# First batch on keys before values, peaks turned on VectorE, and a planner that also counts GpSimd and open banks

## The chip, the cores and the metric

One core of a Trainium2 chip runs the whole kernel. Its engines are named as the profile names them: PE is TensorE's products, PEld its weight loads, DVE is VectorE, ACT is ScalarE, POOL is GpSimd, SP is the SyncE queue that issues DMAs. The metric is the time of one execution in microseconds (us), the median of three runs.

## What is computed

An attention over 32 memory slots feeds a mixture of 8 experts of which each token uses one. The reference, cut to what matters (8 batches, 8 heads, 576 tokens, 64 channels a head; 4608 tokens of 512 channels; experts 512 to 1024 to 512):

```python
a = softmax(phi, axis=2)                    # over the tokens
k_m = einsum('bhsm,bhsd->bhmd', a, k)       # 32 keys and 32 values a head
v_m = einsum('bhsm,bhsd->bhmd', a, v)
x = softmax(q @ k_m.T / 8) @ v_m            # then tokens by 512 channels
logits = x @ w_gate + modality_bias[modality_id]
e = argmax(logits); gate = softmax(logits)[e]
out = gate * (relu(x @ w1[e]) @ w2[e])
```

## The kernel before

**What is multiplied.** The kernel guesses one expert from the biases, takes every token to choose it, and checks that at the end (`verdict`, L539 to L544, sets a flag; the branch behind it, for other choices, isn't taken in the trace). The value products are folded into the expert: for each batch `vw` = values times w1 (L555), so that hidden = relu(a times vw). Large products run in three terms on numbers split into an upper and a lower part (names ending in h and l): `hidden` (L588) takes xh by vwh, xl by vwh, xh by vwl; `outputs` (L617) takes hh by w2h, hl by w2h, hh by w2l. A batch's tokens come in two parts: part 0 has 4 of 9 column groups (tile `xa`, 256 columns), part 1 has 5 (tile `xb`, 320 columns).

**The steps of one batch**, with the lines of the profile:
- `mem_max` folds phi over the tokens on DVE (L253 to L257). `mem_top` turns the result on PE (L141) and reduces it (L268, `topc`). `mem_exp` spreads the peak over the partitions by products with a broadcast weight (L278), subtracts it on DVE (L284) and takes exp on ACT (L287). `mem_sums` adds the exps up, on POOL for all but batch 0.
- `kv_products` multiplies the exps by keys and values together (L307, 72 products, which the trace shows as 144) and by ones (L315, the sums). `kv_divide` divides (L322 to L334), `mem_turn` turns keys and values on PE (L141) and ACT copies them out (L364, L372). `mem_gate` (L391, L396) makes the gate's weights.
- `q_turn` turns queries in place on DVE (L402). `scores` (L414) writes four banks. `soften` and `normalise` (L441 to L473) run on DVE, with one exp on ACT (L449). `a_split` makes xh on ACT (L482) and xl on DVE (L485).
- `logits` (L502 to L514) and `gate` (L521 to L531) give the gates. `gated` (L630) scales a finished output tile on ACT and frees its bank.

**Where things lie.** PSUM has four single banks named `pe`, taken in turn by hidden, outputs and vw, and two pairs named `pair`. A hidden product's bank comes free when ACT (L597) and DVE (L600) have read it. An output tile holds its bank over 24 products and until L630.

**The first batch** is written out by hand in `plan_first`: one list for all engines, with idle products (`warm`, L154 and L156: nothing is read from them) between the steps. All loads go through the SP queue in the order phi, k, v, q (columns of part 0), q (part 1), the modality, the gate's weights, then w1 and w2 of the guessed expert.

**All later batches** are woven by `weave`. It holds two lists, `attention` (each step with a due time, counted in progress of the products) and `experts` (the products), and a table `TAKES` with a time for each kind on PE and a chain on DVE (D), ACT (A) and POOL (P). It simulates one clock and writes out whichever step can go. So the order on each engine is fixed when the program is built, and every engine runs its own list in that order.

Of the kernel before, what the change touches and what calls it, by code (L numbers as in the profile page):

```python
# [54 lines left out]
def attn_moe(ctx: ExitStack, tc: tile.TileContext, q, k, v, phi, mod_id, w_gate, mod_bias, w1, w2, out):  # L55
# [23 lines left out]
    BUSY = 92, 2  # L79
# [69 lines left out]
    def warm(n, small=False, name="pa"):  # L149
        if n > 0:  # L150
            idle = bank(name)
            for _ in range(n):
                if small:
                    nc.tensor.matmul(idle[0:BL, 0:64], lhsT=busy[:, 0:BL], rhs=busy[:, 0:64], start=True, stop=True)  # L154
                else:
                    nc.tensor.matmul(idle, lhsT=busy[:, 0:P], rhs=busy, start=True, stop=True)  # L156
# [113 lines left out]

    def mem_exp(b):
        ph = phs[b % 2].rearrange("p j (c m) -> p j c m", m=M)
        topc = live["topc", b]
        pe = wk.tile([P, HG, QC * M], F32, name="exp")
        px = pe.rearrange("p j (c m) -> p j c m", m=M)
        pb = bank("mem")
        for g in range(NG):
            nc.tensor.matmul(  # L278
                pb[QP * g:QP * (g + 1), 0:P], lhsT=topc[:, g:g + 1].broadcast_to([P, QP]), rhs=ident,
                start=True, stop=True, tile_position=(0, QP * g),  # L280
            )
        peak = pb[:, 0:P].rearrange("p (j o m) -> p j o m", j=HG, o=1)
# [13 lines left out]
    def kv_products(b):  # L296
# [15 lines left out]
        for j in range(HG):  # L312
            for g in range(NG):
# [3 lines left out]
                    start=True, stop=True, tile_position=(QP * g, M * j),  # L317
                )
# [47 lines left out]
    def values_turn(b, fresh=False):  # L366
        if fresh:
            live["pkv"] = pair_of_banks(0)
        turn(live["pkv"][:, 1, 0:P], live["values", b].rearrange("p g d -> p (g d)"))

    def values_out(b):
        nc.scalar.copy(vT[b].rearrange("p j m -> p (j m)"), live["pkv"][:, 1, 0:P])  # L372
# [11 lines left out]
    def first_values():  # L384
        values_turn(0, True)
# [89 lines left out]
    def a_split(b, part, step=None):  # L475
# [9 lines left out]
        nc.vector.tensor_tensor(l, src, h.bitcast(F32), op=ALU.subtract)  # L485
# [164 lines left out]
    def first_w2(c):  # L650
# [11 lines left out]
        "max": (0.0, "D1.9"), "guess": (0.0, "D0.4"), "top": (0.3, "D0.25"),  # L662
        "exp": (0.35, "D1.5 A0.7"), "first exp": (0.35, "D1.5 A0.7"), "first sums": (0.0, "D1.9"), "sums": (0.0, "P0.5"),
        "vwp": (1.15, ""), "vwu": (0.0, "A1.15"), "vwl": (0.0, "D1.35"),
# [422 lines left out]
```

## Time and profile before

| | |
|---|---|
| runs | 403.18, 403.55, 403.67 us, median 403.55 |
| the profiled execution | 405.46 us, of which the span from the first to the last instruction is 403.6 |
| TensorE clock granted | 0.989 of full speed over the span |
| instructions in the span | 10100, of them 4251 products and 4254 weight loads |

The span of the profiled execution is what all rows below count from; the rest of its 405.46 us, 1.9 us, lies outside. A row of the timeline has the start, the time, engine and line, output and inputs, shapes and count; in brackets stands how long the engine had been idle before and what ended it.

### The profile page before, as it was taken

To read this page: it belongs to the slowest core of one execution; us is meant where nothing else is said; L and a number is where in the kernel's file an instruction comes from. 1 tells how busy PE (TensorE), PEld (TensorE's weight loads), DVE (VectorE), ACT (ScalarE), POOL (GpSimd) and SP (SyncE) were. 2 spreads that over 40 slices of the span, in tenths; PEclk is the share of its full clock that TensorE was granted. 3 is DMA by queue.
4 is the path that set the end of the run, shared out by engine and by line. 5 is a ranking of instruction groups with operands and counts; after the bars stand their busy time and mean duration, and the time that the engine had idled before them with its cause. 6 is when DMAs were issued, how large, how long until landed. Compare 5 with 4: busy or idle time off the path is not lost.

```text
span 403.6 us, 10100 instructions
## 1 busy us (share of the span) xinstructions
PE 387.7 (96%) x4251; PEld 309.4 (77%) x4254; DVE 238.8 (59%) x581; ACT 143.7 (36%) x342; POOL 39.9 (10%) x79
## 2 busy tenths in 40 slices
PE   5989998999999999999999999999999999989994
PEld 5448885889678878787968879688877879678983
DVE  2677745975697556853686457764488437860400
ACT  1245333524243324332443315343342424341410
POOL 3158010002000200011000200002000200000000
PEclk9799999999999999999999999999999999999998
DMA  6999158634641491518411282524501011341112
GB/s 218 325 384 392 52 155 298 223 130 112 209 172 54 137 317 65 209 35 294 164 26 54 64 317 86 206 82 110 179 17 38 26 29 28 131 159 26 28 28 58
DMA packets 28966, 56.90 MB, mean 141 GB/s; under 512 B 3312, under 2 KB 8432, under 8 KB 28912
## 3 DMA queue, kind: packets, MB, share of 16 engines
q1 hardware_dynamic: 28624, 56.16, 41.8%
q8 instruction: 35, 0.57, 0.6%
q14 instruction: 19, 0.16, 0.1%
q10 hardware_dynamic: 288, 0.01, 0.0%
HBM read 37.29 MB, written 18.87 MB: 139 GB/s over the span
## 4 chain that ended last, share of the span: by engine, by line
PE 90%; DVE 3%; ACT 2%; DMA 2%; issue 1%; POOL 1%; ACTq 0%; POOLq 0%
PE pe L617 50%; PE pe L588 23%; PE pair L307 4%; PE pe L555 4%; PE pair L414 3%; DMA ph<-in_phi_dram 2%; PE pair L502 1%; PE pair L156 1%; PE pair L141 1%; DVE hl L600 1%; ACT exp L287 1%; PE pair L278 1%; PE pe L156 1%; ACT hh L597 1%; PE pair L555 1%
## 5 line engine op out<-in xcount | busy, mean ns | idle before, releaser
L617 PE MATMUL pe<-w2h,hh 128*128 128x512 f32 x288 | 117.9, 409 | 0.4 <-DVE hl L600 0.4
L617 PE MATMUL pe<-w2h,hl 128*128 128x512 f32 x288 | 112.6, 391 | 0.0
L617 PE MATMUL pe<-w2l,hh 128*128 128x512 f32 x288 | 110.4, 391 | 0.0
L600 DVE SCALAR_TENSOR_TENSOR hl<-pe,hh 128x256 fp32r<-128x256 f32 (+2 forms) x160 | 58.6, 393 | 53.7 <-ACT hh L597 53.2
L617 PEld LDWEIGHTS pe<-w2h,hh 128*128 128x128 f32 x288 | 54.0, 188 | 25.4 <-issue 12.9
L597 ACT ACTIVATE hh<-pe 128x256 fp32r<-128x256 f32 (+2 forms) x160 | 53.6, 361 | 39.5 <-PE pe L588 39.0
L617 PEld LDWEIGHTS pe<-w2l,hh 128*128 128x128 f32 x288 | 54.0, 188 | 12.0
L617 PEld LDWEIGHTS pe<-w2h,hl 128*128 128x128 f32 x288 | 54.2, 188 | 9.3
L630 ACT ACTIVATE ob<-pe,gates 128x512 f32<-128x512 f32 x36 | 24.7, 689 | 82.4 <-PE pe L617 43.1
L588 PE MATMUL pe<-xbh,vwh 128*128 128x320 f32 x128 | 39.8, 311 | 0.0
L588 PE MATMUL pe<-xbl,vwh 128*128 128x320 f32 x128 | 39.6, 309 | 0.0
L588 PE MATMUL pe<-xbh,vwl 128*128 128x320 f32 x128 | 39.5, 309 | 0.0
L588 PE MATMUL pe<-xah,vwh 128*128 128x256 f32 x128 | 36.9, 291 | 0.2 <-DVE hl L600 0.2
L588 PE MATMUL pe<-xal,vwh 128*128 128x256 f32 x128 | 35.9, 283 | 0.0
L588 PE MATMUL pe<-xah,vwl 128*128 128x256 f32 x128 | 35.3, 283 | 0.0
L253 POOL TENSOR_TENSOR t2sums<-exp 128x512 f32<-128x512 f32 x7 | 9.0, 1286 | 261.8 <-ACT exp L287 261.8
L588 PEld LDWEIGHTS pe<-xah,vwh 128*128 128x128 f32 x128 | 24.4, 191 | 1.4 <-DVE hl L600 0.7
L588 PEld LDWEIGHTS pe<-xal,vwh 128*128 128x128 f32 x128 | 24.5, 191 | 0.3
L588 PEld LDWEIGHTS pe<-xbh,vwh 128*128 128x128 f32 x128 | 24.1, 188 | 0.5 <-issue 0.2
L588 PEld LDWEIGHTS pe<-xbl,vwh 128*128 128x128 f32 x128 | 24.1, 188 | 0.3
L588 PEld LDWEIGHTS pe<-xah,vwl 128*128 128x128 f32 x128 | 24.0, 191 | 0.3 <-issue 0.3
L588 PEld LDWEIGHTS pe<-xbh,vwl 128*128 128x128 f32 x128 | 24.1, 188 | 0.0
(117 smaller groups left out, 428.7 us busy)
## 6 DMA issues: line engine op xcount, KB each, us to landing
kv_sb<-in_k_dram SPq DMA_DIRECT2D x8, 1152.0 KB, 5.9
kv_sb<-in_v_dram SPq DMA_DIRECT2D x8, 1152.0 KB, 9.4
out_dram<-ob SPq DMA_DIRECT2D x64, 128.0 KB, 2.4
q_sb<-in_q_dram SPq DMA_DIRECT2D x7, 1152.0 KB, 7.3
ph<-in_phi_dram SPq DMA_DIRECT2D x8, 576.0 KB, 4.0
raw<-in_moe_w_dram SPq DMA_DIRECT2D x2, 1024.0 KB, 8.6
raw<-in_moe_w_dram SPq DMA_DIRECT2D x1, 1280.0 KB, 11.0
out_dram<-ob SPq DMA_DIRECT2D x4, 256.0 KB, 2.0
```

The lines of the kernel that those rows point to most:

```text
L141: nc.tensor.transpose(dst, src, ident[:rows, :rows])
L156: nc.tensor.matmul(idle, lhsT=busy[:, 0:P], rhs=busy, start=True, stop=True)
L253: eng.tensor_tensor(t2, src[:, :, 0:4 * M], src[:, :, 4 * M:8 * M], op=op)
L278: nc.tensor.matmul(pb[QP * g:QP * (g + 1), 0:P], lhsT=topc[:, g:g + 1].broadcast_to([P, QP]), rhs=ident, start=True, stop=True, tile_posit ...
L307: nc.tensor.matmul(live["kvp"][M * j:M * (j + 1), g], lhsT=pe[half, j, c * M:(c + 1) * M], rhs=kv_sb[half, :, j, c * D:(c + 1) * D], start ...
L414: nc.tensor.matmul(sc[g][M * j:M * (j + 1), a, c0 * BL:(c0 + n) * BL].rearrange("p (c t) -> p c t", t=BL), lhsT=kTs[b % 2][p0:p0 + BL, u, ...
L555: nc.tensor.matmul(pvs[g][M * j:M * (j + 1), :], lhsT=vT[b][rows, j, :], rhs=raw1[rows, j, cols], start=True, stop=True, tile_position=(D ...
L588: nc.tensor.matmul(ph[:, 0:n], lhsT=(vl if k == 2 else vh)[:, g, cols], rhs=xl if k == 1 else xh, start=(g == k == 0), stop=(g == NG - 1 a ...
L597: nc.scalar.activation(hs[0][:, f, h0:h0 + p1 - p0], ph[:, p0:p1], AF.Relu)
L600: nc.vector.scalar_tensor_tensor(hl, ph[:, p0:p1], 0.0, hh.bitcast(F32), op0=ALU.max, op1=ALU.subtract)
L617: nc.tensor.matmul(po, lhsT=tile_columns(hl if n == 1 else hh, f, t), rhs=(w2l if n == 2 else w2h)[:, f, :], start=(f == n == 0), stop=(f ...
L630: nc.scalar.activation(ob, po, AF.Copy, scale=gate_of(b, t))
```

## The change

The first part changes the first batch: keys alone (`first_products(0)`, with the sums), then scores of part 0, then values (`first_products(1)`). The queries of part 0 are loaded ahead of the values. The 92 idle products of 64 columns become 224 of 16 columns, and fewer idle products stand between the steps.

```diff
-    BUSY = 92, 2
+    BUSY = 224, 1
...
-        for t in range(2):
-            load_kv(0, t)
+        load_kv(0, 0)
         load_queries(0, 0, RA)
+        load_kv(0, 1)
         load_queries(0, RA, RB)
...
+    def first_products(t):
+        pe, sums = live["pe", 0]
+        pk = None if t else pair_of_banks(1)
+        to = two_banks() if t else [pk[:, g] for g in range(NG)]
...
+        for c in range(QC):
+            for j, g, half in tiles:
+                nc.tensor.matmul(
+                    to[g][M * j:M * (j + 1), 0:D], lhsT=pe[half, j, c * M:(c + 1) * M],
+                    rhs=kv_sb[half, t, j, c * D:(c + 1) * D],
```

The second part changes the peaks of batches 2 to 7: `mem_turn_top`, `mem_swap` and `mem_peak` take the place of the turn on PE, of `topc` and of the four spreading products.

```diff
+    def mem_turn_top(b):
...
+        nc.vector.transpose(tt.rearrange("p j t -> p (j t)"), top)
+        nc.vector.tensor_reduce(tm, tt, axis=AX.X, op=ALU.max)
...
+    def mem_swap(b):
...
+        for a in range(HG):
+            o = a ^ 1
+            nc.gpsimd.tensor_copy(ts_[BL * a:BL * (a + 1)], live["tm"][BL * o:BL * (o + 1)])
...
+    def mem_peak(b):
...
+        nc.vector.tensor_tensor(tm, tm, live["ts"], op=ALU.max)
...
+        nc.vector.tensor_copy(tb, tm.rearrange("p (j o) -> p j o", o=1).broadcast_to([P, HG, BL]))
...
+        nc.vector.transpose(peak.rearrange("p j m -> p (j m)"), tb.rearrange("p j t -> p (j t)"))
```

The third part moves xl from DVE to POOL for all but part 0 of batch 0, and changes the planner: its chains now know POOL, steps on DVE that wait for POOL (T), banks, and how far the instruction count stands in a piece of 256. `vg` and the verdict fall due later. Of the table one line is shown.

```diff
-        nc.vector.tensor_tensor(l, src, h.bitcast(F32), op=ALU.subtract)
+        (nc.gpsimd if b or part else nc.vector).tensor_tensor(l, src, h.bitcast(F32), op=ALU.subtract)
...
-        "xu0": (0.0, "A0.6"), "xl0": (0.0, "D0.75"), "xu1": (0.0, "A0.75"), "xl1": (0.0, "D0.9"),
+        "xu0": (0.0, "A0.6"), "xl00": (0.0, "T0.75"), "xl0": (0.0, "P1.35"), "xu1": (0.0, "A0.75"), "xl1": (0.0, "P1.7"),
...
-            ("vg", [("kvT", b)], mem_gate, 10.4),
+            ("vg", [("kvT", b), ("e", b, 1, 0)], mem_gate, 14.6 if b > 1 else 19.9),
...
-        if b == B - 1:
-            add(("v",), "verdict", [("others", pair)], verdict)
+        if b == B - 1:
+            stage(attention, ("v",), "verdict", [("others", pair)], verdict, due=due + 6.0)
...
-    AHEAD, SPREAD = 4.0, 0.55
+    AHEAD, SPREAD = (6.0, 9.0), 0.55
```

The change has 98 more lines, so a line of before stands further down after it: L141 stays, L402 becomes L479, L441 L518, L485 L562, L568 L645, L588 L665, L617 L694.

Three places show what this moves, all on DVE. The first is the softmax of part 0 of batch 0, where `a` are the scores turned, `sa` and `ra` the sums, and q_sb_99 the queries. Before, from the reciprocal of the keys' sums on:

```order
L324 RECIPROCAL rec<-den 128x2
L402 STREAM_TRANSPOSE q_sb_99<-q_sb_99 128x2x256
L402 STREAM_TRANSPOSE q_sb_99<-q_sb_99 128x2x320 x2
L441 STREAM_TRANSPOSE a<-pair_465 128x256
L445 TENSOR_REDUCE mx<-a 128x8
L447 TENSOR_TENSOR a<-a,mx 128x256
L441 STREAM_TRANSPOSE a<-pair_466 128x256
```

After the change, from the second half of the scores on:

```order
L522 TENSOR_REDUCE mx<-a 128x8
L524 TENSOR_TENSOR a<-a,mx 128x256
L479 STREAM_TRANSPOSE q_sb_99<-q_sb_99 128x2x320
L534 TENSOR_REDUCE sa<-a 128x8 x2
L539 TENSOR_SCALAR sa<-sa 128x16
L540 RECIPROCAL ra<-sa 128x16
L544 TENSOR_TENSOR a<-a,ra 128x512
L550 STREAM_TRANSPOSE aT<-a 128x2x4x32 x2
L562 TENSOR_TENSOR xal<-aT,xah 128x512
L645 TENSOR_TENSOR vwl<-pair_724,vwh 128x512 x2
L479 STREAM_TRANSPOSE q_sb_99<-q_sb_99 128x2x320
L645 TENSOR_TENSOR vwl<-pair_738,vwh 128x512 x2
```

The two turns of part 1's queries (128x2x320) stood ahead of the softmax; now one stands inside it and one between the two halves of vwl.

The second place is the end of part 1 of batch 0, with the gates of its tokens (`lm` to `gates`). Before:

```order
L473 STREAM_TRANSPOSE aT<-a 128x2x5x32 x2
L485 TENSOR_TENSOR xbl<-aT,xbh 128x640
L507 STREAM_TRANSPOSE lgT<-pair_765 128x160
L512 TENSOR_TENSOR lg<-lgT,bias 128x32
L514 TENSOR_TENSOR lg<-lgT,bias 64x8
L521 TENSOR_REDUCE lm<-lg 128x4
L522 TENSOR_TENSOR lg<-lg,lm 128x32
L526 SCALAR_TENSOR_TENSOR first<-lg,rev 128x32
L527 TENSOR_REDUCE fms<-first 128x4
L529 TENSOR_REDUCE se<-ex 128x4
L530 TENSOR_SCALAR se<-se 128x4
L531 RECIPROCAL gates<-se 128x4
```

After:

```order
L544 TENSOR_TENSOR a<-a,ra 128x640
L257 TENSOR_TENSOR t2top<-ph_103 128x512
L258 TENSOR_TENSOR t2top<-t2top 128x4x64
L260 TENSOR_TENSOR top<-t2top 128x128
L261 TENSOR_TENSOR top<-top,ph_103 128x128
L550 STREAM_TRANSPOSE aT<-a 128x2x5x32 x2
L584 STREAM_TRANSPOSE lgT<-pair_965 128x160
L589 TENSOR_TENSOR lg<-lgT,bias 128x32
L591 TENSOR_TENSOR lg<-lgT,bias 64x8
L272 TENSOR_REDUCE topc<-pair_987 128x2
L318 TENSOR_TENSOR exp<-ph_103,pair_992 128x4x160
L318 TENSOR_TENSOR exp<-ph_103,pair_992 128x4x128
```

The maximum of batch 1 now stands ahead of aT, and its `topc` and exp ahead of `lm` to `gates`, which follow the last row shown; xbl has left DVE. On PE, batch 1's turn and spreading products stand between the logits and the first products of part 1.

The third place is the peak of batch 3, in the run of hidden products of batch 2's part 0 (`hl` is L600). Before:

```order
L256 TENSOR_TENSOR top<-t2top 128x128
L257 TENSOR_TENSOR top<-top,ph_103 128x128
L600 SCALAR_TENSOR_TENSOR hl<-pe,hh 128x256 x5
L268 TENSOR_REDUCE topc<-pair_1838 128x2
L600 SCALAR_TENSOR_TENSOR hl<-pe,hh 128x256 x2
L284 TENSOR_TENSOR exp<-ph_103,pair_1861 128x4x160
L284 TENSOR_TENSOR exp<-ph_103,pair_1861 128x4x128
L600 SCALAR_TENSOR_TENSOR hl<-pe,hh 128x256
```

After:

```order
L261 TENSOR_TENSOR top<-top,ph_103 128x128
L279 STREAM_TRANSPOSE tt<-top 128x128
L281 TENSOR_REDUCE tm<-tt 128x4
L677 SCALAR_TENSOR_TENSOR hl<-pe,hh 128x256 x4
L295 TENSOR_TENSOR tm<-tm,ts 128x4
L297 COPY tt<-tm 128x128
L299 STREAM_TRANSPOSE peaks<-tt 128x128
L677 SCALAR_TENSOR_TENSOR hl<-pe,hh 128x256 x4
L318 TENSOR_TENSOR exp<-ph_103,peaks 128x4x160
L318 TENSOR_TENSOR exp<-ph_103,peaks 128x4x128
```

The exp's subtraction moved behind the whole run of hl; the peak no longer comes from a bank, and five small operations of DVE (with four copies on POOL between them) stand for the one reduction.

More of the change, by code (lines that the diff above doesn't have):

```diff
@@ L150, in warm @@
         if n > 0:
-            idle = bank(name)
-            for _ in range(n):
+            idle = pair_of_banks(0) if small else bank(name)
+            for n in range(n):
                 if small:
-                    nc.tensor.matmul(idle[0:BL, 0:64], lhsT=busy[:, 0:BL], rhs=busy[:, 0:64], start=True, stop=True)
+                    r, c = QP * (n % 2), BL * (n // 2 % 4)
+                    nc.tensor.matmul(
+                        idle[c:c + BL, n % 2, 0:16], lhsT=busy[r:r + QP, 0:BL], rhs=busy[r:r + QP, 0:16], start=True, stop=True,
+                        tile_position=(r, c),
+                    )
                 else:
```

172 lines of the change are left out of this document (117 added, 55 removed), and 10 rows, old and new, of the table TAKES.

## The prediction

> **What bounds the kernel now.** I read the page first: the busy times, the rate of transfers by slice of 10 us, and the chain that ended last by engine.
>
> ```profile
> PE 387.7 (96%) x4251; PEld 309.4 (77%) x4254; DVE 238.8 (59%) x581; ACT 143.7 (36%) x342; POOL 39.9 (10%) x79
> GB/s 218 325 384 392 52 155 298 223 130 112 209 172 54 137 317 65 209 35 294 164 26 54 64 317 86 206 82 110 179 17 38 26 29 28 131 159 26 28 28 58
> PE 90%; DVE 3%; ACT 2%; DMA 2%; issue 1%; POOL 1%; ACTq 0%; POOLq 0%
> ```
>
> PE is the bound, with 90% of the chain. So only three things save time: PE work that goes away, PE idle time that goes away, and an earlier start of the real products. The busy times by stretch (start and end, length, PE busy) show where PE idles once these have begun:
>
> ```profile
> 47.83:75.68 27.85, 26.05 (x369) 20.04 (x368) 18.03 (x40) 11.27 (x25) 2.93 (x4) 1.00 0.62 203
> 75.68:126.00 50.32, 50.02 (x553) 40.48 (x552) 36.78 (x95) 19.52 (x49) 2.96 (x4) 1.00 0.47 155
> ```
>
> 1.80 us of idle lie between 47.83 and 75.68, and only 0.30 in the longer stretch behind it. The timeline shows the start:
>
> ```profile
> 1.31 4.75 PE L154 MATMUL pair<-busy 128*32 128x64 bf16 x92 [1.31 <-POOL busy L944]
> 9.69 0.45 PE L141 MATMUL pair<-ident,top 128*128 128x128 f32 x1 [3.20 <-DVE peak L187]
> 11.55 2.74 PE L156 MATMUL pair<-busy 128*128 128x512 bf16 x6
> 12.52 1.25 ACT L287 ACTIVATE exp<-exp 128x640 f32<-128x640 f32 x2 [9.57 <-DVE exp L284]
> 13.81 0.69 DVE L253 TENSOR_TENSOR t2top<-exp 128x512 f32<-128x512 f32 x1 [0.72 <-ACT exp L287]
> 14.22 2.98 PE L307 MATMUL pair<-kv_sb,exp 64*32 64x128 f32 x144
> 15.32 0.29 DVE L257 TENSOR_TENSOR sums<-sums,exp 128x128 f32<-128x128 f32 x1
> 16.60 0.71 DVE L402 STREAM_TRANSPOSE q_sb<-q_sb 128x512 f32<-128x512 f32 x1 [0.99 <-DMA q_sb<-in_q_dram]
> 16.95 0.29 PE L315 MATMUL pair<-ones_c,sums 64*32 64x1 f32 x16
> 17.70 2.33 DVE L402 STREAM_TRANSPOSE q_sb<-q_sb 128x512 f32<-128x512 f32 x3
> 19.45 0.59 PE L156 MATMUL pair<-busy 128*128 128x512 bf16 x2 [0.46 <-ACT kT L364]
> 20.10 1.07 PE L414 MATMUL pair<-q_sb,kT 32*32 32x128 f32 x64
> 21.18 0.45 DVE L441 STREAM_TRANSPOSE a<-pair 128x256 f32<-128x256 f32 x1 [1.16 <-PE pair L414]
> 24.46 0.42 DVE L457 TENSOR_REDUCE sa<-a 128x8 f32<-128x256 f32 x1 [0.15 <-ACT a L449]
> 28.21 2.48 DVE L568 TENSOR_TENSOR vwl<-pair,vwh 128x512 fp32r<-128x512 f32 x4
> 31.26 1.18 PE L414 MATMUL pair<-q_sb,kT 32*32 32x160 f32 x64
> ```
>
> One chain runs through it: peak, exp (ends 13.77), keys and values with their sums, division, scores (20.10), softmax on DVE, hidden products. The second scores at 31.26 need the last vwl, which ends at 30.69, since they write the banks that it reads.
>
> **The first batch, to the scores.** One idle product less stands ahead of the spreading of the peak. Six take 2.74, so one is 0.43 to 0.46, and exp ends near 13.35. Keys and values began 0.45 after exp, behind the sixth idle product; with four left they begin at once: 13.4, 0.8 earlier. For 144 products of half the columns I take 2.1 us, since batch 3 needs 2.25 for 144 of all columns (its row stands below); the other end is 2.98, as here. They end near 15.5. The sums on DVE now stand behind a turn of queries. These land ahead of the values:
>
> ```profile
> kv_sb<-in_v_dram SPq DMA_DIRECT2D x8, 1152.0 KB, 9.4
> ```
>
> 1152 KB at some 350 GB/s (second and third slice) are 3.3 us, so the queries come near 13.3 instead of 16.6 and are turned by 14.0. The four additions took from 13.81 to 15.61, 1.8; now they end near 15.85, and the sums' products near 16.15, against 17.24. From there on one addition more stands in the way (0.2), and two idle products with their gap, 0.65, no longer hold up the scores at 20.10: they start near 18.55, and DVE's `a` near 19.63 instead of 21.18.
>
> **What takes that back.** From `a` to the last vwl DVE took 30.69 - 21.18 = 9.51. Now two turns of part 1's queries are in this list, (2.33 - 0.71) / 2 = 0.81 each; before, they were done while DVE had nothing else, ahead of 21.18. Only 0.15 of them hides behind an exp (the wait in the 24.46 row). 19.63 + 9.51 + 1.47 = 30.6. So the 1.55 are spent: the second scores start near 30.7, a gain of 0.55. PE has then done all 24 first hidden products instead of 22 (0.24), and outputs begin 0.8 earlier than before.
>
> The next rows are of part 1 of batch 0, with one from batch 1 (77.42), and one from the chain of waits (47.99):
>
> ```profile
> 38.37 1.28 POOL L648 TENSOR_TENSOR w2l<-t2sums,w2h 128x512 fp32r<-128x512 f32 x1
> 38.55 1.79 DVE L447 TENSOR_TENSOR a<-a,mx 128x640 f32<-128x640 f32 x1
> 77.42 0.83 DVE L447 TENSOR_TENSOR a<-a,mx 128x640 f32<-128x640 f32 x1
> 42.54 0.83 DVE L467 TENSOR_TENSOR a<-a,ra 128x640 f32<-128x640 f32 x1
> 45.15 0.82 DVE L485 TENSOR_TENSOR xbl<-aT,xbh 128x640 fp32r<-128x640 f32 x1 [0.85 <-ACT xbh L482]
> 46.25 0.35 DVE L507 STREAM_TRANSPOSE lgT<-pair 128x160 f32<-128x160 f32 x1 [0.28 <-PE pair L502]
> 47.83 0.31 PE L588 MATMUL pe<-xbh,vwh 128*128 128x320 f32 x1
> 47.99 5.29 PE pe L588 x36
> 48.05 0.18 DVE L531 RECIPROCAL gates<-se 128x4 f32<-128x4 f32 x1
> 48.33 1.27 ACT L630 ACTIVATE ob<-pe,gates 128x512 f32<-128x512 f32 x2 [0.79 <-DVE gates L531]
> ```
>
> The same subtraction takes 0.83 in batch 1 and 1.79 here, and ends 0.69 behind the end of POOL's operation: 0.96 lost. The Trainium skill, "SBUF — State Buffer", section "SBUF: two separate sides", says that the two engines share a pair of ports as an exclusive lock, so that a VectorE operation with two SBUF inputs blocks while a GpSimd operation that reads SBUF holds it. By that rule, which these rows agree with, moving xl to POOL costs DVE waits; that is the slower rival below.
>
> The 42.54 row would end 0.75 earlier, at 42.6. Then batch 1's maximum (four operations of the sums' shapes, 1.8) comes ahead of aT. From 43.37 to 45.15 aT and xbh took 1.78, about half each; now aT ends near 45.3 and xbh near 46.1. xbl, now on POOL, takes 1.28 for 512 columns by the first row, so 1.6 for 640: 47.8. The logits end near 46.25. Batch 1's topc stands behind lgT and two small additions, about 1.0 in all, so PE's spreading products wait until 47.3, **0.9 us idle**. After them and two outputs, part 1's first hidden products start near 48.3 instead of 47.83.
>
> Next, exp's two subtractions (1.45) stand on DVE ahead of the gates, which take another 1.4 (46.25 to 48.23, without lgT and two additions): gates near 50.6 instead of 48.23. Until ACT scales them by these, two finished output tiles hold two of the four banks. Two hidden tiles (6 x 0.147 each) fill the others by 50.05, and the third waits until ACT frees a bank, near 51.4: **1.35 us idle**. Behind it stand hh and hl of these tiles, and exp's sums on POOL, which run beside it. On the other side, the 1.80 us of idle go, most of it this:
>
> ```profile
> 65.73 0.26 PE L391 MATMUL pair<-wgd,vT 128*32 128x16 f32 x8 [1.24 <-ACT vT L372]
> ```
>
> `vg` stood directly behind the turn that it waits for; now scores, outputs and vw stand between. Batch 1's turn and spreading (0.6, below) are done by then, too. So batch 1's part 0 starts near 48.3 + 27.85 - 1.80 - 0.6 + 1.35 = 75.1 instead of 75.68: **0.6 us gained**; from nothing (a further wait) to 2.9 (neither new wait).
>
> **Batches 2 to 7: the peaks.** Batch 3's, and two rows for the price of products (the last from the chain):
>
> ```profile
> 175.86 0.27 PE L141 MATMUL pair<-ident,top 128*128 128x128 f32 x1
> 177.45 0.44 PE L278 MATMUL pair<-ident,topc 128*64 128x128 f32 x4
> 177.82 0.50 PE L617 MATMUL pe<-w2h,hh 128*128 128x512 f32 x1
> 181.45 2.25 PE L307 MATMUL pair<-kv_sb,exp 64*32 64x128 f32 x144
> 381.78 16.35 PE pe L617 x72
> ```
>
> From 175.86 to 177.82 PE did the turn, six outputs and the spreading: 1.96 us. An output product is 16.35 / 72 = 0.227, so six are 1.36, and a peak costs PE 0.60: six peaks **3.6 us**. At least 0.37 each goes (177.45 to 177.82), 2.2. On DVE two turns and a copy of 128x128 (0.35 each at most, by lgT) and two small operations replace topc, about 1.0 more per batch, while xl leaves, 0.82 for part 1 and less for part 0: no more work than before, and PE hides it. The four copies on POOL are of 32 rows and 4 columns; from 0.1 to 0.3 each, I take 0.2. Peaks have time: only the exp waits for them.
>
> **The rest.** The verdict, and an exp in the chain of waits:
>
> ```profile
> 358.41 0.19 PE L543 MATMUL pair<-ones_c,bad 128*1 128x1 f32 x2 [1.15 <-DVE bad L541]
> 224.08 1.26 ACT exp L287 x2
> ```
>
> PE stands 1.15 us for `bad`, which on DVE follows a hidden tile's hl. After the change the verdict stands 18 outputs (4.1 us) behind the first vw products, and `bad` behind their vwl: **1.2** gone. The exp stood ahead of hh on ACT, so that hidden products went without banks; now it stands behind the whole run. With `vg` of batch 2 I take **1.2** for this over all batches; nothing to 1.9.
>
> **The sum.** 0.6 + 3.6 + 1.2 + 1.2 = 6.6 us. The profiled span is 403.6, its execution 405.46; the runs' median is 403.55. I take the 6.6 off the median: **396.9**.
>
> **The rivals.** *The start keeps its gain*, with neither new wait: 2.3 more, 394.6; 393 with the upper ends of the small terms. For it: topc and gates are late by a microsecond only, by my sum. Against it: their order on DVE. *POOL's lock reaches PE in part*: some 13 xl run on POOL now; if four of them cost PE 0.96 each, 400.8. *Slower*, the same mechanism in every batch: an xl holds a subtraction on DVE, with hl behind it and PE behind hl: 13 x 0.96 = 12.5 more, 409; from seven on the gain is gone. Against it: DVE is busy 59%, and PE has four banks. *The idle products get in the way*: 92 of 64 columns took 4.75, 0.052 each; L307's stood 2.98 / 144 = 0.021 apart, which I take. At 0.021, 224 end at 6.0; from (9.69 - 1.31) / 224 = 0.037 on they hold up the first turn, and at 0.052 by 3.3 us: 400.2. *The change doesn't do what it says*: scores come earlier, but DVE's vwl or w2's landing (the queue is full to 40 us by the GB/s row) sets the products. Then the later 6.0 stay: 397.5, inside my forecast.
>
> **How the numbers follow.** Forecast, 395.5 to 398.5: 50%. The start's gain, 392.5 to 395.5: 21%. Lock in part or idle products, 398.5 to 402.7: 16%. Within 0.2% of before (0.8 us, about what a measurement of this kernel can tell from no change): 4%. Slower: 9%. The range 393.0 to 401.5 leaves out the slower rival and the outer ends of two others, under 2 in 10. Faster 0.87, same 0.04, slower 0.09.
>
> **What would show it.** First scores near 18.5, second near 30.7, DVE without a gap between. PE waiting for topc near 47, an `ob` held by gates near 50.6. Batch 1's part 0 near 75. No PE turn of `top` after batch 1, no wait at the verdict. A subtraction well over 0.83 while POOL writes xl speaks for the lock; if PE then waits for hl, the forecast is wrong.

## The result: 2.5% slower

The changed kernel takes 413.55 us (median of 4, 413.01 to 414.36), the kernel before 403.61 in the same runs (403.18 to 404.01): a ratio of 1.0248, 95% interval 1.0228 to 1.0268. I had forecast 396.9. The page of the profile after, in the lines shown of before, with the line of queue 8 (its one kind of packet is an instruction fetch):

```profile
span 411.6 us, 10639 instructions
PE 381.1 (93%) x4480; PEld 305.5 (74%) x4483; DVE 242.5 (59%) x591; ACT 142.2 (35%) x342; POOL 66.0 (16%) x118
PEclk9958999999999999999999999999999999999998
GB/s 234 355 384 251 117 1 226 314 129 64 254 264 55 27 207 251 127 155 98 357 2 42 103 327 163 131 53 34 250 2 40 39 2 153 130 55 25 28 27 57
q8 instruction: 37, 0.61, 0.7%
PE 80%; DVE 10%; issue 5%; ACT 3%; POOL 0%; ACTq 0%; POOLq 0%; DVEq 0%
```

PE is busy 6.6 us less than before, in a span 8.0 longer. "issue", time in which an engine waited for nothing that the profile shows, has grown from 1% to 5% of the chain. The clock stands at 0.5 and 0.8 of full speed in the third and fourth slice. The time of some landmarks, from the start of the span (e9 and e10 are two of the experiments below):

| start of | before | after | e9: first part alone | e10: two later parts alone |
|---|---|---|---|---|
| first hidden product | 28.36 | 35.77 | 35.70 | 27.66 |
| part 1 of batch 0 | 47.83 | 57.71 | 55.84 | 47.12 |
| part 0 of batch 1 | 75.68 | 86.57 | 82.13 | 74.96 |
| part 0 of batch 7 | 356.39 | 365.54 | 362.60 | 353.36 |
| end of the span | 403.62 | 411.64 | 410.15 | 399.47 |

The loss is made ahead of 86.57: 10.9 us; from there to the end 2.9 are won back. In the profiled execution of before, phi landed at 7.68; in those of the changed kernel, e3, e9, e10 and e11 at 6.13 to 6.26. So the first column is late: e5, whose list is the old one up to 396 us, has phi at 6.06 and the first four of these landmarks at 27.09, 46.55, 74.37 and 354.87, 1.3 to 1.5 us earlier. That is most of the 1.9 us by which the profiled execution of before was above the median. Against e5 the first batch of the changed kernel has lost 8.7 us at its first hidden product, and the loss ahead of 86.57 is 12.2. The timeline of PE after, at its start:

```profile
1.31 1.99 PE L155 MATMUL pair<-busy 64*32 64x16 bf16 x223 [1.31 <-POOL busy L1042]
10.69 0.17 PE L155 MATMUL pair<-busy 64*32 64x16 bf16 x1 [7.39 <-issue]
...
14.54 1.91 PE L363 MATMUL pair<-kv_sb,exp 64*32 64x64 f32 x115
17.58 0.43 PE L363 MATMUL pair<-kv_sb,exp 64*32 64x64 f32 x27 [1.13 <-issue]
...
20.38 1.52 PE L491 MATMUL pair<-q_sb,kT 32*32 32x128 f32 x64 [0.46 <-ACT kT L441]
21.84 0.45 PE L363 MATMUL pe<-kv_sb,exp 64*32 64x64 f32 x13
24.00 2.04 PE L363 MATMUL pe<-kv_sb,exp 64*32 64x64 f32 x128 [1.71 <-issue]
30.19 0.42 PE L363 MATMUL pe<-kv_sb,exp 64*32 64x64 f32 x3 [4.16 <-issue]
```

223 of the 224 idle products run in 1.99 us, 9 ns apart; the last one waits until 10.69, for nothing that the profile shows. The value products are cut into 13, 128 and 3 by two such waits, and take 8.7 us where I had 2.1. Between the waits lie 128 products each time. A product comes with its weight load, so this is 256 instructions, a **piece** below. Queue 8 carries 37 packets of 16 KB in the whole execution; four of them start at 8.08, 15.00, 21.49 and 27.81 and end 1.0 to 1.2 us later, and each of the four waits on PE ends 1.3 to 1.6 us behind such an end. So PE seems to have stood for its own instructions; the experiments test that. In what follows a record is an entry of PE's queue in the trace, a weight load or a wait; the stalls lie at records 226, 355, 485 and 613, some 128 apart.

What follows from it on the engine that I thought was the bound, with two rows of ACT behind it:

```profile
25.28 0.37 DVE L534 TENSOR_REDUCE sa<-a 128x8 f32<-128x256 f32 x1
31.35 0.42 DVE L534 TENSOR_REDUCE sa<-a 128x8 f32<-128x256 f32 x1 [5.69 <-ACT a L526]
```

```profile
30.49 0.52 ACT L389 ACTIVATE values<-pe,rec 128x64 f32<-128x64 f32 x2 [6.72 <-PE pe L363]
30.90 0.42 ACT L526 ACTIVATE a<-a 128x256 f32<-128x256 f32 x1
```

VectorE, on which the prediction let the softmax, the turns and vwl stand without a gap, is idle 5.69 us: the exp that it waits for (L526) stands behind the division of the values (L389) on ACT, and that behind the value products.

### The profile page after: what moved, and what is told of

The parts are those of the page before. It is cut to its first block, busy times and chain, and to the rows that moved or that the text cites. A ratio compares the mean times of both kernels' runs of the same rounds, so it can differ in the third digit from the quotient of the medians.

```text
span 411.6 us, 10639 instructions
## 1 busy us (share of the span) xinstructions
PE 381.1 (93%) x4480; PEld 305.5 (74%) x4483; DVE 242.5 (59%) x591; ACT 142.2 (35%) x342; POOL 66.0 (16%) x118
## 4 chain that ended last, share of the span: by engine, by line
PE 80%; DVE 10%; issue 5%; ACT 3%; POOL 0%; ACTq 0%; POOLq 0%; DVEq 0%
PE pe L694 42%; PE pe L665 23%; PE pair L341 4%; PE pair L491 3%; PE pe L632 3%; DVE vwl L147 1%; PE pair L579 1%; DVE a L544 1%; DVE lg L589 1%; ACT exp L321 1%; DVE aT L550 1%; PE pair L160 1%; PE pair L141 1%; PE pe L363 1%; DVE sa L534 1%
## 5 line engine op out<-in xcount | busy, mean ns | idle before, releaser
L694 PE MATMUL pe<-w2h,hh 128*128 128x512 f32 x288 | 116.9, 406 | 0.0
L694 PE MATMUL pe<-w2h,hl 128*128 128x512 f32 x288 | 112.4, 390 | 0.0
L694 PE MATMUL pe<-w2l,hh 128*128 128x512 f32 x288 | 110.4, 391 | 0.0
L694 PEld LDWEIGHTS pe<-w2h,hh 128*128 128x128 f32 x288 | 54.0, 188 | 24.5 <-issue 12.8
L694 PEld LDWEIGHTS pe<-w2l,hh 128*128 128x128 f32 x288 | 54.0, 188 | 12.0 <-issue 0.2
L694 PEld LDWEIGHTS pe<-w2h,hl 128*128 128x128 f32 x288 | 54.2, 188 | 9.6
L665 PE MATMUL pe<-xbh,vwh 128*128 128x320 f32 x128 | 40.3, 315 | 2.2 <-ACT ob L707 2.2
L665 PE MATMUL pe<-xbl,vwh 128*128 128x320 f32 x128 | 39.5, 309 | 0.0
L665 PE MATMUL pe<-xbh,vwl 128*128 128x320 f32 x128 | 39.5, 309 | 0.0
L665 PE MATMUL pe<-xah,vwh 128*128 128x256 f32 x128 | 36.0, 290 | 2.6 <-ACT ob L707 2.0
L665 PE MATMUL pe<-xal,vwh 128*128 128x256 f32 x128 | 35.0, 283 | 0.0
L665 PE MATMUL pe<-xah,vwl 128*128 128x256 f32 x128 | 35.0, 283 | 0.0
L562 POOL TENSOR_TENSOR xal<-aT,xah 128x512 fp32r<-128x512 f32 x7 | 9.2, 1319 | 153.4 <-ACT xah L559 153.4
L665 PEld LDWEIGHTS pe<-xah,vwh 128*128 128x128 f32 x128 | 24.0, 191 | 4.0 <-ACT ob L707 2.4
L147 DVE TENSOR_TENSOR vwl<-pe,vwh 128x512 fp32r<-128x512 f32 x28 | 17.9, 680 | 14.8 <-ACT vwh L146 14.8
L665 PEld LDWEIGHTS pe<-xbh,vwh 128*128 128x128 f32 x128 | 24.1, 188 | 2.9 <-ACT ob L707 2.5
L146 ACT CAST vwh<-pe 128x512 fp32r<-128x512 f32 x28 | 15.0, 589 | 29.6 <-PE pe L632 29.6
L518 DVE STREAM_TRANSPOSE a<-pair 128x256 f32<-128x256 f32 (+1 forms) x32 | 13.6, 461 | 19.8 <-PE pair L491 19.8
L665 PEld LDWEIGHTS pe<-xbl,vwh 128*128 128x128 f32 x128 | 24.1, 188 | 0.3
```

What stands on the lines that cost most here:

```text
L146: nc.scalar.copy(h, src)
L518: nc.vector.transpose(a[:, g].rearrange("p a c m -> p a (c m)"), sc[g][:, :, RA * part * BL:(RA * part + n) * BL])
L562: (nc.gpsimd if b or part else nc.vector).tensor_tensor(l, src, h.bitcast(F32), op=ALU.subtract)
L665: nc.tensor.matmul(ph[:, 0:n], lhsT=(vl if k == 2 else vh)[:, g, cols], rhs=xl if k == 1 else xh, start=(g == k == 0), stop=(g == NG - 1 a ...
L694: nc.tensor.matmul(po, lhsT=tile_columns(hl if n == 1 else hh, f, t), rhs=(w2l if n == 2 else w2h)[:, f, :], start=(f == n == 0), stop=(f ...
```

## The experiments

Each group of runs shares its runs of the kernel before; the ratio is to these, with its 95% interval.

**e1: the old idle products in the changed kernel.**

```diff
-    BUSY = 224, 1
+    BUSY = 92, 2
...
-    nc.tensor.matmul(idle[c:c + BL, n % 2, 0:16], lhsT=busy[r:r + QP, 0:BL], rhs=busy[r:r + QP, 0:16], ...
+    nc.tensor.matmul(idle[0:BL, 0:64], lhsT=busy[:, 0:BL], rhs=busy[:, 0:64], start=True, stop=True)
```

> The changed kernel with the 92 idle products of 64 columns of before (and the second large one) in place of the 224 of 16 columns: 262 PE instructions fewer ahead of the first turn. Theory 'pieces': PE's instructions come in pieces of 256, each is asked for when PE enters the one ahead of it, and takes 6 to 7 us while the inputs fill the DMA queues; PE stands at the end of a piece until the next is there (records 226, 355, 485 and 613 of PE in the changed kernel, at 10.8, 17.6, 24.0 and 30.2 us). Then the first stall goes (first turn at 9.7 or earlier instead of 11.29), and the later boundaries fall 132 records further on in the program: none of the long stalls inside the key products, one at about the 16th value product, the next at the turn of the values, where PE waits until about 28.8. Second scores near 37 instead of 38.9, total 410.5 to 412. Rival 'idle products only': the whole loss is made ahead of the first turn; everything moves up by 1.6 to 3 us and the value products still take 8.7 us from start to end: 410.5 to 412 with stalls at the same value products. Rival 'order on DVE': the loss comes from DVE's list between the scores: 413.5, value products unchanged.

Measured: 413.44 us (412.42 to 415.0), 1.0243 (1.0205 to 1.0280). Its timeline of PE:

```profile
11.11 1.39 PE L359 MATMUL pair<-kv_sb,exp 64*32 64x64 f32 x118 [0.76 <-ACT exp L317]
14.48 0.54 PE L359 MATMUL pair<-kv_sb,exp 64*32 64x64 f32 x21 [1.98 <-issue]
...
19.13 0.47 PE L359 MATMUL pe<-kv_sb,exp 64*32 64x64 f32 x16
21.32 2.05 PE L359 MATMUL pe<-kv_sb,exp 64*32 64x64 f32 x128 [1.72 <-issue]
27.51 1.01 PE L156 MATMUL pair<-busy 128*128 128x512 bf16 x2 [4.15 <-DVE aT L546]
```

The stall ahead of the first turn is gone (turn at 8.26), and the other boundaries now cut other work: the 118th key product, the 16th value product, and the place right behind the 144th, at records 227, 357 and 485. The last row is put down to a result of VectorE, though the two idle products read none of it; a packet of queue 8 ends at 26.18, 1.3 us ahead of it. The rival, by which the same value products would stall, falls. But I had not expected a stall in the key products, the total is above the 410.5 to 412 that I gave, and the gain does not reach the end: the first hidden product comes 2.6 us earlier than in the changed kernel, part 0 of batch 3 1.5, the end of the profiled execution 1.0. The planner still counts as if the 224 products were there, and batch 2's products of keys and values, with their sums, take 3.13 us here, 0.56 of it a wait for instructions, and 2.21 in the changed kernel.

**e2: the new idle products in the kernel before**, the same edit the other way round.

```diff
-    BUSY = 92, 2
+    BUSY = 224, 1
...
+                    r, c = QP * (n % 2), BL * (n // 2 % 4)
```

> The kernel before with only the 224 idle products of 16 columns in place of its 92 of 64 (and one large one less). 'Pieces': PE stands at record 226 until the piece lands, near 10.8; first turn near 11.3 instead of 9.69; first scores 1.6 later (21.7), 405 to 406.5 in all, since no split of keys and values adds instructions. 'Idle products only' as the whole loss: 3 us or more, 406.5 and up. 'Order on DVE' or 'lock': no part of the loss is here, 403.6.

Measured: 405.27 us (10 runs), 1.0036 (1.0025 to 1.0048).

```profile
1.31 1.99 PE L155 MATMUL pair<-busy 64*32 64x16 bf16 x223 [1.31 <-POOL busy L948]
9.59 0.17 PE L155 MATMUL pair<-busy 64*32 64x16 bf16 x1 [6.29 <-issue]
```

As the theory of pieces has it: the same 224th product stalls, up to 9.59 where I had 10.8, the first turn comes at 10.20, and this part of the change costs 1.4 us.

**e3: the first batch of before, all else as changed.** `plan_first`, loads, idle products and the first hidden products of before; peaks, xl, planner, `vg` and verdict of the change, with the start value of the planner's instruction count set anew.

```diff
-        load_kv(0, 0)
+        for t in range(2):
+            load_kv(0, t)
         load_queries(0, 0, RA)
-        load_kv(0, 1)
...
-        add(("k", 0), "k0", [("exp", 0)], first_products, 0, floor=10.8)
+        add(("kv", 0), "kv0", [("exp", 0)], kv_products, 0, floor=11.7)
...
-        count = 350
+        count = 126
```

> The changed kernel with the first batch of before (keys and values together, its loads, its idle products, its order), and all later parts of the change: peaks on VectorE, xl on POOL, the planner, vg and verdict later. 'Pieces': the first batch runs as before (first scores 20.1, second 31.3); the later parts keep what they gain in the changed kernel's trace, 1.7 over batches 2 to 7 and 1.5 in the last, less 1.0 in part 1 of batch 0: 399.5 to 402.5. 'Lock' or 'order on DVE later': the later parts lose, 404 or more.

Measured: 408.49 us (406.17 to 410.0), 1.0094 (1.0064 to 1.0124). I was wrong on this one. The start is as I expected, or better (hidden products at 27.06), but the later parts lose. PE idles 1.6 for `topc` and 2.2 for a bank in part 1 of batch 0; and batch 3's keys and values take 4.11 us with their sums, 2.21 undisturbed, 1.7 of it a wait for instructions. This profiled execution is the slowest of the five. So the later parts are no gain by themselves in this plan: with the old first batch they cost 4.7 us.

**e4: xl on VectorE again, in the changed kernel.**

```diff
-        (nc.gpsimd if b or part else nc.vector).tensor_tensor(l, src, h.bitcast(F32), op=ALU.subtract)
+        nc.vector.tensor_tensor(l, src, h.bitcast(F32), op=ALU.subtract)
...
-        "xl0": (0.0, "P1.35"), "xl1": (0.0, "P1.7"),
+        "xl0": (0.0, "D0.75"), "xl1": (0.0, "D0.9"),
```

> The changed kernel with xl on VectorE in all batches (and so told to the planner). 'Lock' (xl on POOL holds VectorE's operations with two inputs in SBUF): 2 to 12 us faster than the changed kernel, 402 to 411. 'Pieces': no part of the loss is here, 413.5 within 1.5.

Measured: 414.78 us, 1.0263 (1.0240 to 1.0286), no faster than the changed kernel. The lock is there all the same. The groups of the small addition of the biases to the logits, of the changed kernel and of this run, where xl is on VectorE:

```profile
L589 DVE TENSOR_TENSOR lg<-lgT,bias 128x32 f32<-128x32 f32 x8 | 7.0, 870 | 0.3
```

```profile
L589 DVE TENSOR_TENSOR lg<-lgT,bias 128x32 f32<-128x32 f32 x8 | 1.5, 192 | 0.3
```

Eight small operations take 870 ns each with xl on POOL, and 192 without. It is VectorE's time, and the total is no better without it.

**e5: the price of a piece by itself.** 640 of the new idle products behind the last output product of the kernel before.

```diff
         weave()
+        last = pair_of_banks(0)
+        for n in range(640):
+            r, c = QP * (n % 2), BL * (n // 2 % 4)
+            nc.tensor.matmul(last[c:c + BL, n % 2, 0:16], lhsT=busy[r:r + QP, 0:BL], rhs=busy[r:r + QP, 0:16], ...
```

> The kernel before with 640 idle products of 16 columns put behind the last output product, where few DMAs run; nothing reads them. It measures the price of a piece by itself: 640 products and their weight loads are five pieces of 256 instructions. In the changed kernel a piece takes 6.2 to 6.8 us from entering the one before it, while inputs arrive. Theory 'pieces behind other DMAs': with quiet queues a piece takes well under that, 1.5 to 3 us, so PE stands 1 us or less at each boundary, and the 640 end 10 us or so after their start. Rival 'a piece always takes that long': the boundaries lie 6 us apart here too, and the 640 take some 25 to 30 us.

```profile
396.52 1.43 PE L971 MATMUL pair<-busy 64*32 64x16 bf16 x159
400.07 1.17 PE L971 MATMUL pair<-busy 64*32 64x16 bf16 x128 [2.12 <-issue]
403.52 1.20 PE L971 MATMUL pair<-busy 64*32 64x16 bf16 x128 [2.28 <-issue]
406.98 1.20 PE L971 MATMUL pair<-busy 64*32 64x16 bf16 x128 [2.26 <-issue]
410.43 0.94 PE L971 MATMUL pair<-busy 64*32 64x16 bf16 x97 [2.26 <-issue]
```

This is one execution of 419.05 us, and only its tail is read. With quiet queues a piece takes 3.46 us from start to start, about half of the 6.2 to 6.8 at the start. That is more than the 1.5 to 3 that I expected, and PE stood 2.1 to 2.3 at each boundary where I had 1 or less. So even then PE can't run more than 256 instructions in 3.46 us once it has used up what was fetched ahead.

**e6: half of the new idle products**, in the changed kernel.

```diff
-    BUSY = 224, 1
+    BUSY = 112, 1
```

> The changed kernel with 112 idle products of 16 columns in place of 224. All boundaries fall 112 PE records further on in the program. 'Pieces': none ahead of the first turn (8 to 9.7 us instead of 11.29); one at about the 112th key product; one at about the 8th value product, where PE stands until 19.5 to 21; one at about the 138th value product, where it stands until 26 to 27.5, in place of 30.2. Second scores at 34 to 36 (38.9 with 224, 36.3 with 92 of 64 columns); 409 to 412. Rival 'few instructions, no stall': value products in 2 us as the key products, second scores near 31: 405 to 407. Rival 'order on DVE': second scores stay near 38, 413.

Measured: 413.73 us (411.75 to 415.16), 1.0241 (1.0196 to 1.0286).

```profile
14.64 0.69 PE L363 MATMUL pair<-kv_sb,exp 64*32 64x64 f32 x45 [1.68 <-issue]
...
21.43 0.63 PE L491 MATMUL pair<-q_sb,kT 32*32 32x128 f32 x3 [2.77 <-issue]
21.99 2.02 PE L363 MATMUL pe<-kv_sb,exp 64*32 64x64 f32 x125
27.62 0.64 PE L363 MATMUL pe<-kv_sb,exp 64*32 64x64 f32 x19 [3.62 <-issue]
```

The boundaries are where the theory had them within 13 products (the 99th key product, the 61st product of the scores, the 125th value product) and the last two stalls end at 21.43 and 27.62, a little behind the 19.5 to 21 and 26 to 27.5 that I had. The hidden products start 1.7 us earlier than with 224. The total is no better, and above my 409 to 412: the boundaries of all later batches have moved too, and the planner does not know of it. Batch 3's products of keys and values, with their sums, took 3.68 us here and 2.21 in the changed kernel; and the clock, at full speed there from 33.6 on, was at half speed again from 60.0 to 63.4, behind PE's wait for a bank (2.5 between two weight loads, up to 59.84).

**e7: batch 1's steps due as before**, in the changed kernel.

```diff
-    plan_memory(1, 2.9, floor=27.5)
+    plan_memory(1, 5.9, floor=27.5)
```

with `top`, `exp`, `sums` and `vg` of batch 1 due 1.5, 3.0, 3.2 and 10.4 behind, and `vg` again without its wait for the softmax of part 1.

> The changed kernel with batch 1's memory steps due as before (5.9 after the start of the products instead of 2.9, top, exp and sums 1.5, 3.0 and 3.2 behind, gate at 10.4). Theory 'batch 1's steps in DVE's list': PE's wait for topc (1.5) and for the two output banks held by the late gates (2.2) go, so from the second scores to batch 1's part 0 it takes 3 to 3.7 us less: 410 to 411. Rival: something else is late there (POOL's xl, w2): the time stays at 413.5.

Measured: 414.43 us, 1.0273 (1.0255 to 1.0292). The waits for `topc` and for the two late outputs are gone, and others stand in their place (PE's waits between 55 and 95 us):

```profile
PE pe L665 <- ACT xah L559: 2.4, 1, 2.4
PE pe L665 <- POOL xal L562: 1.0, 1, 1.0
PE pair L468 <- ACT vT L449: 0.9, 1, 0.9
```

So it isn't these due times alone. e9 has none of these waits: the old planner with the new first batch needs 46.4 us from the first hidden product to batch 1's part 0, the new one 50.8 (before: 47.3). What of the new planner's rules makes the difference is left open.

**e8: two later parts alone.** The kernel before, with the peaks of batches 2 to 7 by `mem_turn_top`, `mem_swap` and `mem_peak`, and the verdict due 6.0 later.

```diff
+            ("ttop", [("max", b)], mem_turn_top, 0.8),
+            ("swap", [("ttop", b)], mem_swap, 1.0),
+            ("top", [("swap", b)], mem_peak, 2.0),
...
-            add(("v",), "verdict", [("others", pair)], verdict)
+            stage(attention, ("v",), "verdict", [("others", pair)], verdict, due=due + 6.0)
```

> The kernel before with two later parts of the change alone: the peaks of batches 2 to 7 on VectorE and POOL, and the verdict later; first batch, xl, batch 1's steps and the rest of the planner as before. Theory: the verdict's wait (1.15) goes, and 0.37 to 0.4 of PE a peak, 2.3: 400.0 to 401.5. Rival 'the five small operations on VectorE delay hl': nothing gained by the peaks, 402.5. Rival 'lock by the four copies on POOL': 403.8 or more.

Measured: 408.45 us, 1.0116 (1.0098 to 1.0134), far from what I expected. It lies in the open range of one rival, POOL's four copies as a lock; but these take 0.84 us in all and end at 91.99 for batch 2, whose peak comes at 100.93, and e10 keeps them for five batches and gains. Two readings. From batch 3's first hidden product, 175.07, to batch 7's, 359.94, it takes 184.87 us, before 186.70 (169.69 to 356.39): the four peaks in between, of batches 4 to 7, save 1.83, **0.46 each** on average. (My expectation of e10 counts five there and has 0.37.) But from part 1 of batch 1 to part 0 of batch 2 it takes 38.97 instead of 31.97:

```profile
102.99 2.25 PE L337 MATMUL pair<-kv_sb,exp 64*32 64x128 f32 x144 [0.87 <-ACT exp L317]
106.79 0.27 PE L345 MATMUL pair<-ones_c,sums 64*32 64x1 f32 x16 [1.55 <-POOL sums L257]
108.71 0.44 PE L141 MATMUL pair<-ident,keys 128*128 128x128 f32 x2 [1.65 <-ACT values L362]
```

Batch 2's exp on ACT starts at 102.20, before at 95.08; PE, which used to do the peak and so came to the keys when exp and sums were done, now waits for exp, for the sums on POOL and for the division in turn, and the clock is at half speed from 109.2 to 116.1. And the verdict, 6.0 later, still stood ahead of its input: its wait of 1.1 is unchanged.

**e9: the first part alone.** The kernel before, with the new `plan_first`, loads, idle products and first hidden products.

```diff
-        add(("kv", 0), "kv0", [("exp", 0)], kv_products, 0, floor=11.7)
+        add(("k", 0), "k0", [("exp", 0)], first_products, 0, floor=10.8)
...
+        add(("v", 0), "v0", [("exp", 0)], first_products, 1, floor=15.2)
```

> The kernel before with the first part of the change alone: keys ahead of values, its loads, its idle products and its order; peaks, xl, batch 1's steps, the planner and the verdict as before. 'Pieces' as the main cause: PE stands at records 226, 355, 485 and 613 as in the changed kernel, value products end near 30.5, second scores near 38.9; 410 to 413. Rival 'the two halves share the loss': 406 to 408.

Measured: 411.27 us (410.94 to 412.0), 1.0180 (1.0166 to 1.0195). The stalls are at the same records and times as in the changed kernel, within 0.01 us. **The first part alone costs 7.3 us of the 9.9.**

**e10: e8 mended.** Peaks on VectorE for batches 3 to 7 only, and the verdict due 14.0 later.

```diff
-        if b > 1:
+        if b > 2:
             peak = live["peak", b].rearrange("p j (o m) -> p j o m", o=1)
...
+        if b == B - 1:
+            stage(attention, ("v",), "verdict", [("others", pair)], verdict, due=due + 14.0)
```

> The kernel before with two later parts of the change, mended: peaks on VectorE and POOL for batches 3 to 7 only (batch 2's stays on PE, so that its exp and sums come when they did), and the verdict's product well behind its inputs (it stands among the last output products ahead of part 1 of the last batch). By the run with all six peaks a peak is worth 0.37, five are 1.8, and the verdict's wait 1.15: 2.5 to 3 us faster than before, 400.5 to 401.5. Rival: a new plan moves other steps into waits: 403 or more.

Measured: **401.19 us** (6 runs, 399.8 to 401.49) against 403.93 (11 runs), 0.9925 (0.9911 to 0.9939): 2.7 us faster than the kernel before. Busy times by stretch, of before and of e10 (start and end, length, PE busy first), from batch 1's part 0 to batch 7's, and on to the last output:

```profile
75.68:356.39 280.71, 279.84 (x3081) 225.37 (x3080) 182.65 (x449) 105.25 (x252) 17.64 (x24) 1.00 0.38 127
356.39:398.12 41.73, 40.58 (x219) 35.30 (x217) 8.79 (x28) 10.50 (x29) 0.00 (x0) 1.00 0.15 37
```

```profile
74.96:353.36 278.40, 276.14 (x3057) 223.95 (x3055) 187.23 (x469) 105.14 (x252) 21.23 (x44) 1.00 0.38 128
353.36:393.93 40.57, 40.57 (x219) 35.15 (x217) 8.77 (x28) 10.53 (x29) 0.00 (x0) 1.00 0.16 38
```

2.31 us in the first stretch, in which five peaks lie (0.46 each, as in e8), and 1.16 in the second, where PE's idle time is now nothing: the verdict.

**e11: the other loads out of the way.** In the changed kernel, `guess` loads w1 alone; the loads of w2, of phi and keys of batch 1 stand behind the load of batch 1's values, which waits for the value products.

```diff
-            load_kv(1, 0)
             load_kv(1, 1)
+            guess_w2()
+            load_kv(1, 0)
             load_queries(1)
```

> The changed kernel with the loads of w2, of phi of batch 1 and of the keys of batch 1 behind the load of the values of batch 1 on the SP queue, which waits for the value products. So hardly any input moves from 23.3 us, when w1 has landed, until the value products end; all else is later for it, and the total says nothing. 'Pieces behind other DMAs': PE enters the piece at record 485 at 24.0 as before, and gets the next one after some 3.5 to 4.5 us, not 6.2: record 613 runs at 27.5 to 28.5 instead of 30.19. Rival 'another thing makes a piece slow at the start, such as the cold clock': 30.2.

```profile
21.36 0.33 PE L366 MATMUL pe<-kv_sb,exp 64*32 64x64 f32 x13
23.70 1.79 PE L366 MATMUL pe<-kv_sb,exp 64*32 64x64 f32 x128 [2.01 <-issue]
27.15 0.42 PE L366 MATMUL pe<-kv_sb,exp 64*32 64x64 f32 x3 [1.66 <-issue]
```

w1 landed at 23.30, the next load was issued at 27.60. The piece that took 6.19 us in the changed kernel takes 3.45, the same as in the quiet tail of e5. Its fetch starts at 24.84, 1.1 us after PE has entered the piece ahead, against 3.8 in the changed kernel. The clock was at half speed from 24.4 to 31.2, as in the changed kernel from 19.9 to 33.6, so the cold clock isn't the reason. What makes this piece slow in the changed kernel are the inputs in the DMA queues. The total, 413.06 in one execution, says nothing, since the inputs come late.

**e12: the second exp ahead of the division of the values**, in the changed kernel's lists of ACT and VectorE; PE's list is the same.

```diff
+        add(("e", 0, 0, 1), "e", [], soften, 0, 0, None, 1)
         add(("vn", 0), "vn0", [("v", 0)], first_divide, 1)
         add(("more", 0), "nothing", [], more_keys, 0)
-        add(("e", 0, 0, 1), "e", [], soften, 0, 0, None, 1)
```

> The changed kernel with the exp of the second half of the first scores ahead of the division of the values on ACT, so that VectorE's softmax runs on while PE waits for its instructions (it stood 5.7 us, up to 31.35). PE's list is the same. 'Pieces': the value products still end near 30.5, and vw, vwl and the second scores need them; only what VectorE has to do between comes earlier: first hidden product 34.5 to 35.2 instead of 35.77, second scores 37.5 to 38.5 instead of 38.90, 412.5 to 413.5. Rival 'the order on ACT and VectorE is the cause': second scores near 33 to 34, 408 to 409.

Measured: 412.86 us (411.06 to 414.71), 1.0230 (1.0191 to 1.0269). Its profiled execution is the fastest of the four, and all of PE's start lies 1.6 us earlier in it (the first stall ends at 9.15 instead of 10.79), though PE's list is the same. From the end of the last stall to the first hidden product it takes 5.58, as in the changed kernel (30.19 to 35.77), though the attention's weights are now turned at 26.3; VectorE then idles 8.07 instead of 5.69. The order on ACT isn't the cause.

## Why the prediction was wrong

It failed at the price of the 144 value products, and of the idle ones: both were costed by rows of products alone, "0.021 apart" and "2.1 us", and in neither did I ask where PE's instructions come from. By the runs a piece of 256 instructions takes 3.46 us from start to start when queues are quiet (e5, 3.45 in e11) and 6.2 to 6.8 while the inputs land, and its fetch begins only when PE has entered the piece ahead. The change adds 262 instructions ahead of the first turn (131 products more, with their loads) and 288 by the split (144 products more), more than two pieces in the 30 us in which they are slowest. The first part alone loses 7.3 us (e9). That all of this is the stalls isn't shown by a total: no run has the new order without them, and e1 and e6, which shorten them, lose their gain in later batches.

A second step failed: the later parts were to give 6.0 of the 6.6 us, and the sum puts no loss against them. With the old first batch they cost 4.7 (e3), and behind the new one about 2.6 (9.9 less 7.3), so the two losses do not simply add. With the new first batch the loss is made between the first hidden product and batch 1's part 0, where the new list needs 50.8 us and the old planner's 46.4. Part of it is the two waits in part 1 of batch 0, below; which of the planner's rules does the rest stays open.

Point by point:
- **Idle products.** I feared 0.052 us apiece and took 0.021; they took 0.009. They got in the way for the reverse reason, being too quick for their instructions. Price: 1.4 alone (e2).
- **First scores** at 18.55: 20.38. Without the stall ahead of the first turn they came at 17.68 (e1) and 17.62 (e6); against e5's 18.86, the old list with phi as early, a gain of 1.2 where I had 1.55. That the times are within 0.9 of the forecast is in part luck: phi landed 1.4 earlier there than in the profile that I worked from (6.25 and 6.28 against 7.68), and a stall of 1.7 to 2.0 in the key products, which the sum lacks, took most of that back.
- **Second scores** at 30.7, bound by VectorE's list: 38.90, bound by the value products, which end 8.7 us after their start. The two turns of queries that I had as the price cost little: one is done before the stall, and PE waits 0.25 for the vwl behind the other. "A further wait" was in the bounds of this part with nothing gained; 8 us of loss were not.
- **Part 1 of batch 0.** The two waits are where I saw them, and larger. These rows are of PE, then of VectorE (`se` of the gates) and POOL:

```profile
56.78 0.44 PE L312 MATMUL pair<-ident,topc 128*64 128x128 f32 x4 [1.13 <-DVE topc L272]
61.86 0.41 PE L665 MATMUL pe<-xbh,vwh 128*128 128x320 f32 x1 [2.23 <-ACT ob L707]
```

```profile
59.76 1.06 DVE L607 TENSOR_SCALAR se<-se 128x4 f32<-128x4 f32 x1
```

```profile
59.52 1.26 POOL L257 TENSOR_TENSOR t2sums<-exp 128x512 f32<-128x512 f32 x1 [3.12 <-ACT ex L601]
```

  1.13 for 0.9, and 2.23 for 1.35. Most of the second excess is one small operation of the gates, 1.06 us where its neighbours take 0.18, which ends with POOL's first addition of the exps. I had the lock as a rival for xl, and had put the sums "beside" the gates at no cost.
- **Peaks**, 3.6: 0.46 each on average (e8, e10), 2.8 for six, between my 0.60 and the 0.37 that I named as sure. The 0.60 took all that the six outputs between turn and spreading don't fill at 0.227 apiece; by their starts these six took 1.56 (0.26 apiece), turn and spreading 0.03 and 0.37. The rows from 175.86 to 181.45 that I called batch 3's are batch 4's, between products of batch 3; the sum takes their price for all six.
- **Exp out of the hidden runs and vg**, 1.2: not for exp. I had read the new order at batch 3, and it isn't that of batches 4 and 6: there exp stands ahead of a finished output and of hh on ACT, and 24 hidden products take 4.23 us instead of 2.9. ACT in batch 6:

```profile
322.37 1.26 ACT L321 ACTIVATE exp<-exp 128x640 f32<-128x640 f32 x2 [5.19 <-DVE exp L318]
323.54 0.67 ACT L707 ACTIVATE ob<-pe,gates 128x512 f32<-128x512 f32 x1
324.11 0.92 ACT L674 ACTIVATE hh<-pe 128x256 fp32r<-128x256 f32 x3
```

  Together with the peaks, batches 1 to 6 gave 1.74 (280.71 to 278.97, part 0 of batch 1 to part 0 of batch 7) for 4.8. The wait for `vT` behind the turn is gone, as foretold.
- **Verdict**, 1.2: right. From batch 7's part 0 to the last output 40.21 us against 41.73, and 1.16 less in e10 by the verdict alone.
- **The rivals.** POOL's lock on xl did not make it slower: VectorE has the time (e4). 15 xl run on POOL, not some 13. The upper ends of the small terms give 393.9, where I wrote 393. That the first part alone loses was none of the rivals.

The Trainium skill, "Runtime: NRT & Kernel Launch", section "Instruction fetch mechanics", says that instructions come in blocks of 256 by a queue of the engine's own, and that the cost of crossing into the next block is mostly hidden. The block's size agrees with the 128 products between the waits; the second part doesn't hold here: 2.1 to 2.3 us of stall a block in e5, and up to 7.39 at the start.

## What to carry to other kernels

Many small products in a row are priced by instructions, not by columns: count them between two points of the list, in pieces of 256, before moving or splitting anything, most of all while the inputs of the kernel fill the DMA queues. Edits ahead of a tuned plan move all later boundaries with them, so a gain at the start can be lost batches later (e1, e6). When a step is taken off PE, check what PE was covering by it, and whether the next steps are then late: e8 and e10 differ by one batch's peak and the verdict's place, and by 7 us.

## What the runs showed that I had not expected

- An engine's own instruction stream can be the bound: 3.46 us a piece in quiet, 6.2 to 6.8 with 230 to 380 GB/s of inputs moving.
- The fetch of a piece begins about 1.1 us after PE has entered the one ahead of it when nothing else is queued (e5, e11), 3.8 to 4.2 at the start; the packet takes about 1.1; PE goes on some 1.3 later.
- 16-column products on alternating positions of the array run 9 ns apart, their loads too, as long as instructions last (223 in 1.99 us).
- In six of the profiles (e1, e3, e4, e6, e8, e11) the clock fell back to half speed for 3.4 or 6.8 us at a time in the middle of the products, behind waits of PE in the early batches.
